# A two-part table of w1's last rows, loaded straight into the matmul operand, in a conv and mixture-of-experts kernel

## The chip, the cores and the metric

The kernel runs on one core of a Trainium2 chip. Its engines work side by side, each on its own row of instructions: PE (TensorE, matmuls), DVE (VectorE), ACT (ScalarE), POOL (GpSimd) and SP (SyncE, which here only issues DMAs). The metric is the device time of one execution in microseconds, as the median of several runs. Beside the runs stands one profiled execution, whose trace gives the rows of this document.

## What is computed

Shapes: x is (8, 2880, 192), so 23040 tokens of 192 values; `w_group` (192, 4), `w_expert` (4, 192, 4), `w1` (4, 4, 192, 1024), `w2` (4, 4, 1024, 192), all float32. Cut to what matters, the reference is:

```python
w = softmax(weight_gen)                        # 8 heads, 7 taps per token
x = einsum('bshk,bskhg->bshg', w, windows(x))  # causal convolution, then (23040, 192)
g = argmax(x @ w_group)                        # one of 4 groups per token
e = argmax(x @ w_expert[g])                    # one of 4 experts in it
h = maximum(x @ w1[g, e], 0)
out = p_group * p_expert * (h @ w2[g, e])      # the two softmax values of the choice
```

Every token goes to exactly one of 16 experts.

## The kernel before

**The front.** The tokens lie in 180 columns of 128, in 15 groups of 12. For each chunk of 6 columns DVE computes the softmax of the taps (L265 `m`, L267 and L268 for the exponential, L273 to L279) and the products of the convolution (L294 `pr`), and sums them (L312, L330); in the first six chunks PE sums part of them by matmuls with the identity (L335), which ACT takes out of PSUM (L338 `xrow`). Then come the router's logits (PE L392, L393, L375, L419; ACT L385 `rem`, L399 `xT`, L411, L422 `ls`), the choice of group and expert on DVE (from L346 `mxg` to L449 `oh`; ACT L352 for the exponentials), the ranks of tokens within an expert (PE L459, L460), and the scatter of each token's row into the DRAM table `rows` by POOL (L503, a DMA per column).

**The blocks.** After certain groups (14 rounds) DVE builds a table that names for each block the rows and the expert. A block takes tokens of one expert. The first ten are plain (128 tokens, float32 matmuls); then come two-unit blocks of 256 tokens; after the last group ten wide blocks of 384, six of 256 and two plain ones. For each block SP loads the rows (`xb`, L779), w1 (L790 for plain blocks: two DMAs straight into the operand `wa`; L792 and L799 for the others) and w2 (`wc`, L803). PE transposes `xb` (L872, L881, L882), multiplies with w1 (L907, the first gemm) and w2 (L945 and L947, L948, the second); ACT takes relu (`hh`, L913; L918 for the split form) and the output (`y`, L954); POOL scatters `y` to the output (L962).

**Split operands.** In blocks that are not plain a float32 operand is written as a rounded high half and a low half in the type float32r, and the gemm is a sum of products of halves. w1 has 192 rows per expert. Its first 128 are loaded as `raw0` (512 KB); ACT casts them into part 0 of `wa` (L816) and DVE writes the difference into part 1 (L840). Part 2 of `wa` holds the last 64 rows twice: 64 partitions with the high half, 64 with the low half. Before the change it is made from `raw1`, to which SP loads 64 rows of w1 and 64 rows of the DRAM table `w1lo` (two DMAs of 256 KB, L799), by one ACT cast (L825, function `split`, part 2).

**The table.** `w1lo` is built in the opening, while the front runs, by the generator `halves` (L595 to L620), pair by pair of experts, k = 0 to 7. For each pair SP fetches the 2 x 64 rows (two DMAs of 256 KB, L610) into a tile that is not yet needed otherwise (parts of `wa`, `wc` and raw tiles); ACT writes minus the high half into another such tile (L602); SP writes the raw tile to `w1lo` (512 KB, L604); POOL adds the negative high half to it with an accumulating DMA (L605). The steps are placed in the program at the planned times `HALVES`, 36 to 78 us; the fetch of pair k stands ahead of the write of pair k-1.

**What sets the order.** Within PE, ACT, DVE and SP the order is that in which the program is written: a planner with a cost for each step steps through blocks (`blocks`) and, where its clock says there is room, through the front and `halves`. An engine takes its row in order, so an instruction that waits holds up all behind it. SP's DMAs also share eight completion counters in turn, so that each waits for the one eight places ahead of it on SP to land. Rings of tiles (three of `wa`, four of `wc`, two each of `raw0` and `raw1`, one `raw2` for w2 of the split blocks) make a load wait until the last reader of that tile is done. `ask(n, part)` puts a load on the list of wanted ones (part 0 `xb`, 1 and 2 w1, 3 w2), `pump` issues them, `pieces(n)` lists a block's ACT casts. The low halves of relu (`hl`, written behind L918 in the split blocks) lie in six pieces of the front's `pr` tiles, taken in turn, so the front has to be complete before the first such block.

## Time and profile before

| | |
|---|---|
| runs | 1208.67, 1213.08, 1214.5 us |
| median | 1213.08 us |
| profiled execution | 1211.98 us |
| its span on the core | 1210.3 us |
| mean granted clock of PE | 0.983 of full speed |
| PE busy | 1135.7 us, 94% of the span |
| DVE busy | 961.3 us, 79% |
| ACT busy | 651.7 us, 54% |
| POOL busy | 571.1 us, 47% |
| DMA | 275.08 MB, mean 227 GB/s |

The profile's page gives busy times of each engine, the span in 40 slices, the chain of work that ended last, and groups of instructions by line; the trace behind it answers narrower questions (what an engine waited for, a timeline of one engine, busy times in given windows). The span is the time from the first to the last instruction on the core; the execution's own time is 1.7 us longer. A name like L825 is a line of the kernel before.

### The profile page before, as it was taken

How to read it: one execution, taken by the hardware profiler on the slowest of the kernel's cores; microseconds unless marked ns; L12 is line 12 of the kernel's file. 1: busy time of each engine (PE TensorE's matmuls, PEld its weight loads, DVE VectorE, ACT ScalarE, POOL GpSimd, SP SyncE). 2: the span in 40 equal slices, each digit the busy share in tenths (PEclk: the TensorE clock that was granted, in tenths of full speed). 3: DMA queues.
4: the chain of work that ended last, by engine and by line, in shares of the span. 5: the costliest groups of instructions: out<-in, count | busy, mean ns of one | idle time of the engine just before them, and what ended most of it. 6: DMA issues, size and time to landing. Idle time of an engine off the chain costs nothing.

```text
span 1210.3 us, 24473 instructions
## 1 busy us (share of the span) xinstructions
PE 1135.7 (94%) x8357; PEld 1078.7 (89%) x8357; DVE 961.3 (79%) x1646; ACT 651.7 (54%) x1235; POOL 571.1 (47%) x608
## 2 busy tenths in 40 slices
PE   5787798999999999999999999999999899999995
PEld 2444788999999999999999999999999899999995
DVE  8899887999998999899999899897625656665560
ACT  1332344655655655655665655555556666666651
POOL 6154182846174747675647664475654112222221
PEclk9998898999999999999999999999999999999998
DMA  5797699787878877888787878649687755555660
GB/s 170 223 303 224 226 298 311 221 296 230 255 252 263 275 238 226 278 261 258 215 283 249 265 223 292 198 129 296 199 275 229 218 155 157 159 163 161 196 204 17
DMA packets 82758, 275.08 MB, mean 227 GB/s; under 512 B 15063, under 2 KB 31734, under 8 KB 80832
## 3 DMA queue, kind: packets, MB, share of 16 engines
q1 hardware_dynamic: 62296, 229.76, 60.9%
q0 software_dynamic: 20208, 43.39, 11.4%
q8 instruction: 67, 1.10, 0.4%
q14 instruction: 67, 0.55, 0.2%
q10 hardware_dynamic: 120, 0.28, 0.1%
HBM read 225.83 MB, written 48.42 MB: 227 GB/s over the span
## 4 chain that ended last, share of the span: by engine, by line
PE 59%; issue 20%; DVE 7%; DMA 6%; POOL 4%; ACT 1%; SPq 1%; POOLq 1%; DVEq 0%; ACTq 0%
PE py L945 26%; PE ph L907 25%; POOL out L962 4%; DVE pr L294 3%; PE pl L375 2%; DMA wt<-in_weight_gen 1%; DMA out<-y,xb 1%; PE tpx L882 1%; PE tpx L881 1%; DMA w1lo<-raw 1%; PE ph L335 1%; DMA raw<-w1lo 1%; PE tp L392 1%; DMA xin<-in_x 1%; DMA raw<-in_moe_w 1%
## 5 line engine op out<-in xcount | busy, mean ns | idle before, releaser
L907 PE MATMUL ph<-xh,wa 128*128 128x256 f32 (+1 forms) x1992 | 466.2, 307 | 0.0
L962 POOL DMA_INDIRECT out<-y,xb x189 | 208.1, 1101 | 445.6 <-DVE y L960 202.5
L945 PE MATMUL py<-wc,hh 128*128 128x192 f32 x2160 | 402.1, 327 | 3.2 <-ACT y L954 3.2
L907 PE MATMUL ph<-xl,wa 128*128 128x256 f32 (+1 forms) x1328 | 360.6, 290 | 0.0
L945 PEld LDWEIGHTS py<-wc,hh 128*128 128x128 f32 x2160 | 348.4, 191 | 3.4 <-ACT y L954 3.4
L907 PEld LDWEIGHTS ph<-xh,wa 128*128 128x128 f32 x1992 | 338.1, 190 | 3.3 <-issue 1.8
L913 ACT ACTIVATE hh<-ph 128x512 f32<-128x512 f32 (+2 forms) x296 | 165.4, 560 | 265.9 <-PE ph L907 265.8
L294 DVE TENSOR_TENSOR pr<-xin,wt 128x1152 f32<-128x1152 f32 x186 | 249.2, 1352 | 5.5 <-PE py L335 3.5
L907 PEld LDWEIGHTS ph<-xl,wa 128*128 128x128 f32 x1328 | 252.3, 190 | 0.4 <-DVE xl L840 0.3
L503 POOL DMA_INDIRECT rows<-xrow,ix x156 | 224.7, 1441 | 47.3 <-POOL ix L502 34.5
L312 DVE TENSOR_TENSOR xrow<-xrow,pr 128x1152 f32<-128x1152 f32 x144 | 194.9, 1353 | 0.7
L840 DVE SCALAR_TENSOR_TENSOR pr<-ph,hh 128x384 fp32r<-128x384 f32 (+1 forms) x128 | 77.6, 607 | 101.7 <-ACT hh L918 100.6
L840 DVE TENSOR_TENSOR wa<-raw,wa 128x1024 fp32r<-128x1024 f32 x83 | 101.5, 1223 | 33.1 <-ACT wa L816 31.4
L947 PE MATMUL py<-wc,hh 128*128 128x384 f32 x352 | 111.9, 365 | 0.0
L918 ACT ACTIVATE hh<-ph 128x384 fp32r<-128x384 f32 (+1 forms) x128 | 68.5, 535 | 73.9 <-PE ph L907 73.9
L502 POOL COPY ix<-posi 128x1 int32<-128x1 int32 x156 | 71.8, 472 | 66.6 <-DMA rows<-xrow,ix 39.3
L816 ACT CAST wa<-raw 128x1024 fp32r<-128x1024 f32 x83 | 87.2, 1050 | 4.2 <-DMA raw<-in_moe_w 4.2
L948 PE MATMUL py<-wc,pr 128*128 128x192 f32 x352 | 88.5, 251 | 0.0
L825 ACT CAST wa<-raw 128x1024 fp32r<-128x1024 f32 x83 | 86.7, 1044 | 0.4 <-DMA raw<-w1lo 0.4
L954 ACT ACTIVATE y<-py,xb 128x192 f32<-128x192 f32 x179 | 67.3, 423 | 22.1 <-PE py L945 20.4
L840 DVE TENSOR_TENSOR xl<-tpx,xh 128x512 fp32r<-128x512 f32 (+1 forms) x94 | 61.7, 656 | 17.2 <-ACT xh L887 16.1
L948 PEld LDWEIGHTS py<-wc,pr 128*128 128x128 f32 x352 | 67.8, 193 | 0.0
(178 smaller groups left out, 1343.5 us busy)
## 6 DMA issues: line engine op xcount, KB each, us to landing
wc<-in_moe_w SPq DMA_DIRECT2D x73, 768.0 KB
raw<-in_moe_w SPq DMA_DIRECT2D x83, 512.0 KB
xin<-in_x SPq DMA_DIRECT2D x14, 1728.0 KB
raw<-in_moe_w SPq DMA_DIRECT2D x91, 256.0 KB
raw<-w1lo SPq DMA_DIRECT2D x83, 256.0 KB
raw<-in_moe_w SPq DMA_DIRECT2D x22, 768.0 KB
xb<-rows SPq DMA_DIRECT2D x72, 194.0 KB
wa<-in_moe_w SPq DMA_DIRECT2D x24, 384.0 KB
```

The source lines that it names most:

```text
L294: nc.vector.tensor_tensor(out=dst, in0=o.xin[:, c0 + k:c0 + k + SC, :].rearrange("p s (h g) -> p s h g", g=HG), in1=w4[:, c0:c0 + SC, :, k ...
L312: nc.vector.tensor_tensor(out=acc, in0=acc, in1=prs[k - 2], op=ALU.add)
L503: written_once(nc.gpsimd.indirect_dma_start(out=rows[:, :], out_offset=bass.IndirectOffsetOnAxis(ap=ix, axis=0), in_=src, in_offset=None, ...
L816: nc.scalar.copy(out=o.wa[:, 0, :], in_=o.raw[0])
L825: nc.scalar.copy(out=o.wa[:, 2, :], in_=o.raw[1])
L840: f(*a, **k)
L907: nc.tensor.matmul(ph[:, v, :], lhsT=w[:, f0:f0 + P], rhs=rhs, start=i == 0, stop=i == len(terms) - 1)
L913: nc.scalar.activation(out=hh, in_=ph, func=AF.Relu)
L945: nc.tensor.matmul(b.acc[t], lhsT=hh[:, v, c], rhs=wc[0][:, f, :], start=f == 0 and not (b.wide and t == 1), stop=f == NFT - 1 and not (b. ...
L947: nc.tensor.matmul(b.py[t], lhsT=hh[:, v, c], rhs=wc[f // 4][:, f % 4].rearrange("p l d -> p (l d)"), start=f == 0, stop=False)
L948: nc.tensor.matmul(b.acc[t], lhsT=hl[:, v, c], rhs=wc[f // 4][:, f % 4, 0, :], start=False, stop=f == NFT - 1)
L962: ins = nc.gpsimd.indirect_dma_start(out=out[:, :], out_offset=bass.IndirectOffsetOnAxis(ap=b.x.bitcast(I32)[:, t, D + 1:D + 2], axis=0), ...
```

## The change

The DRAM table becomes `w1s`, with two parts of 64 rows for each expert: part 0 the rounded high half, part 1 the low half. For each pair `halves` now makes two casts on ACT (minus the high half, then the high half, L592 of the changed kernel), writes each in two DMAs of 256 KB, one for each expert (L595), and adds the raw rows to the low part by two accumulating DMAs on POOL (L597), whose target is of type float32r. More tiles serve as places meanwhile: all three `wa`, the four `wc`, both `raw0` and one of the former raw2. A non-plain block loads the 128 x 1024 of both parts with one DMA of 512 KB straight into part 2 of `wa` (L789); L825 and the ring `raw1` go. That load is asked for at the end of block n for block n+3 (for the third block of all in the lead) and not behind the casts of the block two ahead, and its tile is free when PE has done the first gemm of block n. `hl` gets a ring of four tiles of its own, and the front is forced to completion only ahead of wide split blocks.

```diff
-    w1lo = dram.tile([NE, HP, F], F32, name="w1lo")
+    w1s = dram.tile([NE, 2, HP, F], F32, name="w1s")
...
-    hls = []
-
-    def new_hl():
-        if not hls:
-            for _ in range(3):
-                t = cv.tile([P, 2, 2, BK], F32R, name="pr", bufs=3)
-                hls.extend(t[:, k] for k in range(2))
-        hls.append(hls.pop(0))
-        return hls[-1]
-
-    new_raw = [ring(f"raw{i}", m, [P, n]) for i, (n, m) in enumerate(((F, 2), (F, 2), (NFT * D, 1)))]
+    new_raw = [ring(f"raw{i}", m, [P, n]) for i, (n, m) in enumerate(((F, 2), (NFT * D, 1)))]
+    new_hl = ring("hl", 4, [P, 2, BK], F32R)
...
-        def lower_half(k):
-            e, hi, raw = 2 * k, his[k % len(his)], raws[k]
-            nc.scalar.activation(out=hi, in_=raw, func=AF.Copy, scale=-1.0)
-            low = w1lo[e:e + 2].rearrange("e p f -> (e p) f")
-            nc.sync.dma_start(out=low, in_=raw)
-            nc.gpsimd.dma_start(out=low, in_=hi.bitcast(F32), accum_op=ALU.add)
-            run("pool", 1.1, run("act", 1.0))
+        spare, third, other = [wp.tile([P, 3, F], F32, name="wa", bufs=3) for _ in range(3)]
+        raws = [t[:, k, :] for t in (spare, third) for k in range(3)] + [new_raw[0]() for _ in range(2)]
+        first3 = [other[:, k, :] for k in range(3)]
+        rest5 = [wp.tile([P, NFT, D], F32, name="wc", bufs=4).rearrange("p f d -> p (f d)")[:, 0:F] for _ in range(4)]
+        rest5.append(new_raw[1]()[:, 0:F])
+        parts = [t.bitcast(F32R) for t in 2 * first3 + 2 * rest5]
+
+        def divide(k):
+            for q, scale in enumerate((-1.0, 1.0)):
+                part = parts[2 * k + q]
+                nc.scalar.activation(out=part, in_=raws[k], func=AF.Copy, scale=scale)
+                run("act", 1.0)
+                for h in range(2):
+                    nc.sync.dma_start(out=w1s[2 * k + h, 1 - q], in_=part.bitcast(F32)[h * HP:(h + 1) * HP, :])
+            for h in range(2):
+                nc.gpsimd.dma_start(out=w1s.bitcast(F32R)[2 * k + h, 1], in_=raws[k][h * HP:(h + 1) * HP, :], accum_op=ALU.add)
+            run("pool", 2.2, clk["act"])
...
-            for h, src in enumerate((w1v[bass.ds(o.ev, 1), P:D, :], w1lo[bass.ds(o.ev, 1), :, :])):
-                nc.sync.dma_start(out=o.raw[1][h * HP:(h + 1) * HP, :], in_=src.rearrange("o p f -> p (o f)"))
+            nc.sync.dma_start(out=new_wa(o, F32R).bitcast(F32)[:, 2, :], in_=w1s[bass.ds(o.ev, 1)].rearrange("o l p f -> (o l p) f"))
...
-        elif part == 2:
-            nc.scalar.copy(out=o.wa[:, 2, :], in_=o.raw[1])
-            o.tw = max(o.tw, run("act", 0.95))
...
-        return [(1, 1), (2, 1)] + ([] if whole(n) else [(3, 0), (3, 1)])
+        return [(1, 1)] + ([] if whole(n) else [(3, 0), (3, 1)])
...
-            if not o.whole:
+            if b.wide and not o.whole:
                 while step() is not False:
                     pass
...
             if plain(n):
                 ask_w(n)
+            else:
+                ask(n, 2)
             ask_x(n)
...
-                if end and n + 3 < n1 and (plain(n + 3) or plain(n + 2)):
-                    ask_w(n + 3)
-                    if not plain(n + 3):
-                        ask_w(n + 4)
+                if end and n + 3 < n1:
+                    if plain(n + 3):
+                        ask_w(n + 3)
+                    else:
+                        ask(n + 3, 2)
+                        if plain(n + 2):
+                            ask(n + 3, 1)
+                            ask(n + 4, 1)
```

On SP, the building of the table in the opening (targets of L610 are places for fetched rows; here the fetches of pairs 4, 5 and 6 and the writes of pairs 3, 4 and 5) stood thus in the kernel before:

```order
L610 DMA raw_190<-in_moe_w 64x1024 x2
L604 DMA w1lo<-wc 128x1024
L610 DMA raw_189<-in_moe_w 64x1024 x2
L604 DMA w1lo<-raw_190 128x1024
L610 DMA raw_192<-in_moe_w 64x1024 x2
L604 DMA w1lo<-raw_189 128x1024
```

and stands thus in the changed one, where L602 is the fetch (pairs 5, 6 and 7) and L595 the write (pairs 4 and 5):

```order
L602 DMA wa<-in_moe_w 64x1024 x2
L595 DMA w1s<-wc 64x1024 x4
L602 DMA raw_190<-in_moe_w 64x1024 x2
L595 DMA w1s<-raw_191 64x1024 x2
L595 DMA w1s<-wc 64x1024 x2
L602 DMA raw_189<-in_moe_w 64x1024 x2
```

One write per pair, from the fetched tile, has become four from the tiles that ACT writes, and each fetch stands behind them.

On ACT, between the logits' copies of the second chunk (L399) and the evacuation of the third chunk's sums (L338), before:

```order
L399 COPY xT<-tp 128x384
L602 ACTIVATE wc<-raw_190 128x1024
L602 ACTIVATE wc<-raw_189 128x1024
L602 ACTIVATE wc<-raw_192 128x1024
L338 COPY xrow<-py_584 128x2x192
L338 COPY xrow<-tpx 128x2x192
L338 COPY xrow<-ph_586 128x2x192
```

and after, where the lines are L390, L592 and L329:

```order
L390 COPY xT<-tp 128x384
L592 ACTIVATE wc<-wa 128x1024 x2
L592 ACTIVATE raw_191<-wa 128x1024
L592 ACTIVATE wc<-wa 128x1024
L592 ACTIVATE wc<-raw_190 128x1024 x2
L329 COPY xrow<-py_607 128x2x192
L329 COPY xrow<-tpx 128x2x192
L329 COPY xrow<-ph_609 128x2x192
```

Ahead of the third chunk's evacuation there are six casts, of pairs 4, 5 and 6, where there were three.

On SP, at the first two-unit block (block 10: `raw_189`; block 11: `raw_190`), before:

```order
L792 DMA raw_189<-in_moe_w 128x1024
L799 ISA
L799 DMA raw_191<-in_moe_w 64x1024
L799 ISA
L799 DMA raw_191<-w1lo 64x1024
L787 TENSOR_LOAD tab_1368
L787 ISA x2
L792 ISA
L792 DMA raw_190<-in_moe_w 128x1024
```

and after, where L783 loads the first 128 rows and L789 the table:

```order
L789 ISA
L789 DMA wa<-w1s 128x1024
L783 ISA
L783 DMA raw_189<-in_moe_w 128x1024
L778 TENSOR_LOAD tab_1411
L778 ISA x2
L783 ISA
L783 DMA raw_190<-in_moe_w 128x1024
```

The table's load for block 10, with `wa` as its target, has come ahead of `raw_189`, and the two loads to `raw_191` and `raw_192` are gone. At the end of the table's building, pair 7's write (behind the second plain block's loads) has become four writes; its tiles are no longer parts of the `wa` that the third plain block's load takes.

## Rows read from the trace of the kernel before

**Rows 1.** The page: busy time of each engine over the span

```profile
PE 1135.7 (94%) x8357; PEld 1078.7 (89%) x8357; DVE 961.3 (79%) x1646; ACT 651.7 (54%) x1235; POOL 571.1 (47%) x608
```

**Rows 2.** Windows: busy us of each engine (instructions), granted clock, DMA share, GB/s

```profile
60.00:90.00 30.00, 25.04 (x123) 13.90 (x122) 27.34 (x41) 11.82 (x22) 16.80 (x16) 0.94 1.04 305
...
300.00:840.00 540.00, 539.89 (x4271) 532.69 (x4271) 496.87 (x840) 318.05 (x594) 308.24 (x295) 1.00 0.78 248
840.00:1140.00 300.00, 291.85 (x2028) 285.28 (x2027) 171.28 (x334) 183.97 (x342) 98.35 (x117) 0.99 0.64 192
```

**Rows 3.** What PE waits for, 125 to 215 us: total, times, longest

```profile
PE py L945 <- ACT y L954: 3.2, 1, 3.2
PE pl L459 <- DVE oh L449: 3.0, 1, 3.0
```

**Rows 4.** The page's groups: busy, mean ns of one, idle before, releaser

```profile
L825 ACT CAST wa<-raw 128x1024 fp32r<-128x1024 f32 x83 | 86.7, 1044 | 0.4 <-DMA raw<-w1lo 0.4
```

**Rows 5.** Timeline of PE, 960 to 968 us: start, duration, what [idle before]

```profile
966.54 0.45 PE L881 MATMUL tpx<-ident,xb 128*128 128x128 f32 x1 [3.47 <-DVE xl L840]
```

**Rows 6.** Timeline of ACT in the opening

```profile
47.99 1.06 ACT L602 ACTIVATE wa<-wa 128x1024 fp32r<-128x1024 f32 x1
...
67.88 2.01 ACT L602 ACTIVATE wc<-raw 128x1024 fp32r<-128x1024 f32 x2
...
76.67 0.48 ACT L338 COPY xrow<-py 128x384 f32<-128x384 f32 x1 [5.54 <-PE py L335]
...
83.40 0.36 ACT L422 COPY ls<-pl 128x240 f32<-128x240 f32 x1 [0.64 <-PE pl L419]
```

**Rows 7.** The chain of work that ended last: start, duration, what

```profile
83.67 1.36 DVE pr L330
...
100.07 11.14 DMA w1lo<-raw
...
111.77 5.96 DMA w1lo<-wa
...
120.66 6.72 DMA wt<-in_weight_gen
```

**Rows 8.** Timeline of SP (its DMA issues), pairs 3 to 6 of the table

```profile
49.73 1.29 SPq L610 DMA_DIRECT2D wc<-in_moe_w  x2
...
55.05 0.34 SPq L604 DMA_DIRECT2D w1lo<-wc  x1
55.43 1.39 SPq L610 DMA_DIRECT2D raw<-in_moe_w  x2
...
60.65 1.66 SPq L610 DMA_DIRECT2D raw<-in_moe_w  x2
65.97 0.34 SPq L604 DMA_DIRECT2D w1lo<-raw  x1
...
70.05 0.34 SPq L604 DMA_DIRECT2D w1lo<-raw  x1
```

**Rows 9.** Timeline of SP around the third plain block's load

```profile
111.90 1.51 SPq L779 DMA_DIRECT2D xb<-rows  x2
117.93 0.90 SPq L790 DMA_DIRECT2D wa<-in_moe_w  x2
```

**Rows 10.** Timeline of DVE, 121 to 129 us

```profile
127.41 0.85 DVE L265 TENSOR_REDUCE m<-wt 128x96 f32<-128x672 f32 x1 [4.92 <-DMA wt<-in_weight_gen]
```

**Rows 11.** Windows at the two places where PE has stood

```profile
143.00:149.00 6.00, 5.97 (x26) 5.93 (x26) 5.62 (x25) 1.26 (x4) 1.18 (x3) 0.50 0.00 1
198.00:200.00 2.00, 1.60 (x5) 1.60 (x6) 1.97 (x7) 1.64 (x4) 0.97 (x1) 0.50 1.05 284
```

**Rows 12.** Timeline of SP at the first two-unit block

```profile
186.97 0.33 SPq L792 DMA_DIRECT2D raw<-in_moe_w  x1
```

**Rows 13.** Timeline of ACT at the first two-unit block

```profile
196.45 1.04 ACT L816 CAST wa<-raw 128x1024 fp32r<-128x1024 f32 x1 [4.20 <-DMA raw<-in_moe_w]
```

**Rows 14.** Timeline of PE: block 7's last first-gemm group

```profile
188.88 1.06 PE L907 MATMUL ph<-xd,wa 96*128 96x128 f32 x8
```

21 lines of the change are left out of this document (6 added, 15 removed).

## The prediction

> **What bounds the kernel now.** I read the busy times of the engines first, then a table of windows, then who waits for whom where TensorE (PE) stands, then the queues around those places. ScalarE (ACT), which the change relieves most, is busy 54% of the span, PE 94% [rows 1]. From 300 to 840 us PE is busy 539.89 of 540 us, and from 840 to 1140 us 291.85 of 300 [rows 2]: in these 840 us all of PE's gaps together are 8.3 us, and work taken from ACT or from the queues can win no more than that there. The gaps lie before 300 us. From 60 to 90 us PE is busy 25 of 30 us, VectorE (DVE) 27.34, and the DMA engines are full at 305 GB/s [rows 2]: this opening is a chain on DVE with the DMA rings full beside it. What the change can do to the time is decided by the opening, and by two places where PE stands about 3 us each: at 143.03 us for DVE's `oh`, and at 198.40 us for ACT's `y` [rows 3].
>
> A warning on this reading. The Trainium skill's page "Perfetto Trace Analysis" (section "Identifying the Most-Contended Engine") says that busy matmuls are no good measure of the headroom of TensorE, and that one should look at the busy share of its weight loads. By that column PE is loading 532.69 of 540 us here, so that up to 7 us would be open, and 6.6 us more from 840 to 1140. By my reading the term for these stretches is nothing; by the page's it is bounded by -14 us, all of it won. I stay with the row of PE, since the list of its waits names almost nobody there; the page's case is among the rivals.
>
> **What goes: 83 casts and 83 loads.** Each non-plain block loses L825, 1044 ns on ACT, 86.7 us in all [rows 4]. ACT has the room, and PE doesn't wait for it from 300 us on, so this counts nothing where PE is full; the cover is PE's own work. It counts where a block stands just behind such a cast: at 966.54 us, the one large stop late in the kernel, PE waits 3.47 us for `xl` behind DVE [rows 5]; L825 goes shortly ahead of the ACT steps that DVE waits for there, but most of the 3.5 us is L816, the subtraction and the wide block's first preparation. I take -0.2, with 0 and -1.0 as ends (the whole cast). The two 256 KB loads of a block become one of 512 KB: the bytes are the same, the issues on SP fewer.
>
> **What the opening pays.** Per pair k of experts the table now costs two ACT casts (before one), four writes of 256 KB on SP (before one of 512 KB) and two accumulating DMAs on POOL (before one): 8 casts, 24 SP DMAs, 8 POOL DMAs and 4 MB of writes more. The casts lie on ACT, 1.06 us each [rows 6], which is nowhere full; the POOL DMAs stand between scatters that keep pace with the rows, and I put them at nothing, with 2 us as the other end if the last scatter of the first table slips. What matters is order. Before, SP wrote a raw tile as soon as it was fetched; now a write waits for the cast on ACT, and SP asks for the fetch of pair k+2 behind the writes of pair k. So the even pairs form a chain: two casts (2.1 us), four issues (about 1.5 us), a fetch of L us, again. Pair 0's casts can begin where ACT has its first one now, at 47.99 us [rows 6]. Pair 6's then begin at 48.0 + 3 x (3.6 + L) and end 2.1 us later, and behind them in ACT's order stands the evacuation of the third chunk's sums, now at 76.67 us [rows 6]. Behind that are the logits, out at 83.40 + 0.36 = 83.76 us [rows 6], and DVE takes them when its L330 ends at 83.67 + 1.36 = 85.03 us [rows 7]: 1.27 us of slack. The delay of the DVE chain is thus D = 48.0 + 10.8 + 3L + 2.1 - 76.67 - 1.27 = 3L - 17, not less than about 0.7, since pair 4's casts don't begin before 67.88 us [rows 6].
>
> L is read from SP's rows, from the issue of a fetch to the write that waits for its landing: 49.73 to 55.05 (5.3 us), 55.43 to 65.97 (10.5) and 60.65 to 70.05 (9.4) [rows 8]. At L = 5.3 D is 0.7, at 10.5 it would be 14.5. I take L = 7.5, somewhat under the mean of the three (8.4), because SP now stands while ACT casts, and the rings are emptier when the fetch is asked for; against that, 1 MB of writes is queued just ahead of it, which with its own 0.5 MB is 5.2 us at the 305 GB/s of [rows 2]. So D = 5.5, between 0.7 and 10. Everything behind (the first table, the scatters, the first plain loads) shifts by D; there is no idle time of DVE to take it up before 127 us.
>
> **What the stop at 143 us gives back.** Pair 7's write, issued at 100.07, takes 11.14 us to land, its accumulation from 111.77 another 5.96 [rows 7]. The third plain block's load goes to the tile that this accumulation reads, so SP, which has issued `xb` at 111.90, stands until 117.93 [rows 9]; behind it is the load of `wt` at 120.66, 6.72 us to land [rows 7], for which DVE stands 4.92 us until 127.41 [rows 10]. That ends in the 3.0 us for which PE stands before 143.03 [rows 3], and PE then runs from 143 to 149 at a granted clock of 0.50, 1.2 of its 2.4 GHz [rows 11]: it does in 6 us what takes half of that at full clock. After the change pair 7's parts lie in other tiles, so the load may go right behind `xb`, at about 113.5: 4.4 us earlier, and `oh` with it (DVE is free 4.9 us before it starts). PE itself is ready for `oh` 3.0 us earlier. So the stop of 3.0 us goes, and with it about 3.3 us of half clock: -6.3. If only half of that is won (PE late itself, clock low for another reason) it is -3.
>
> **What the first two-unit block pays.** `raw0` of block 10 is issued at 186.97 [rows 12] and ACT's cast of it starts at 196.45, after 4.20 us of waiting for it [rows 13]; `hh`, `xd` and `y` stand behind the cast and PE behind `y` (3.19 us, [rows 3]). In the new order `w1s` of block 10 comes ahead of `raw0`, and it waits on SP for PE's last first-gemm group of block 7, at 188.88 to 189.9 [rows 14]. The rings are full there (1.05, 284 GB/s from 198 to 200, [rows 11]), so the later issue itself costs little, but 512 KB stand ahead that did not: 0.52 / 284 = 1.8 us. I take +1.8; 0 if the backlog drains earlier, +3 if the issue (2.9 us later) counts in full. The Trainium skill's "DMA: Bandwidth & Descriptors" (section "Bandwidth") measured 341 GB/s for a transfer of 1 MB: by that the same 512 KB are 1.5 us and the sum 0.3 less; the row is slower, and I keep it.
>
> **Later blocks.** `w1s` of block n+3 is asked for when block n ends and waits for the tile that block n's first gemm gives up. The slowest landing read above took 11.14 us [rows 7], and two blocks lie between the request and the need (83 non-plain blocks in the thousand us behind 200 are some twelve us each): nothing. If the cover were gone, each of 83 blocks would pay. The four tiles of `hl` cost nothing: the front's steps stand in the same order until the first group's last blocks.
>
> **Sum** against the profiled execution, 1211.98 us (span 1210.3): +5.5 - 6.3 + 1.8 - 0.2 = +0.8. The median of the three runs is 1.1 us above the profiled one, so 1213.08 + 0.8 = 1213.9, rounded to 1214.
>
> **Rivals.** (1) Slower: the opening. SP, ACT and the fetches go round in a circle, and ACT stands on pair 6's fetch in front of the evacuation. The place is the third chunk, the price D - 4.7 in all (the other terms as above), and it is slower by more than 6 us from D = 10.8, or L = 9.3. For it: two of the three fetches read took longer than that, and 4 MB are added to full rings (13 us at 305 GB/s). Against: fewer bytes are in flight, since no more than a pair's writes stand ahead. L = 9.3 to 10.5 gives +6.2 to +9.8, say 1221. (2) Faster: the opening costs 1 us, since the fetches are short, and the stop at 198 us goes too, because SP is no longer 4.4 us late and has one request less in the way: +1 - 6.3 - 3.2 and half of another 3.3 us of half clock (the window from 198 to 200 is at 0.50), so -10, to about 1204. For it: both stops hang on late loads; against: `raw0` stands behind a wait for PE that it did not have. (3) The page's case: PE's weight loads gain from a freer ACT over 840 us. All of it would be -14, to about 1200; against it, PE waits for no ACT step there. (4) The change doesn't bite late: a `w1s` load lands after its block starts. 0.5 us in each of 83 blocks is +41, about 1255; against it stand two blocks of lead. (5) Nothing moves, because D eats just what the stop gives: that is inside the forecast.
>
> **How the numbers follow.** Forecast, with D between 0.7 and 10 and its neighbours at their ends: 1207 to 1219, chance 0.58. Rival 1: 0.23. Rival 2: 0.14. Rival 3: 0.02. Rival 4: 0.03. 0.5%, about what a measurement of this kernel can tell from no change, is 6 us, so faster means under 1207 and slower over 1219. Faster: rivals 2 and 3 and the low end of the forecast, 0.18. Slower: rivals 1 and 4, 0.26. The range reaches from the low end of the forecast to rival 1's end: 1206 to 1222.
>
> **What would show it.** In the profile after: pair 6's two casts on ACT shortly ahead of the third chunk's evacuation, at 81 to 84 us instead of 70; `mxg` of that chunk about 5 us late; SP not standing between `xb` and the third plain load; no wait of PE for `oh` behind it and no 0.50 there; at the first two-unit block a wait of PE for `y` of about 5 us; PE full from 300 to 840 us as before; no L825. It would be wrong if the third chunk's evacuation hardly moves (then faster), if DVE waits for `xin` or scatters in the opening, if the stop at 143 us merely changes its cause, or if PE waits for `w1s` in block after block.

## The result and the profile after

The changed kernel takes 1221.65 us (median of 4 runs, 1221.13 to 1225.47) against 1210.88 us for the kernel before (4 runs, 1206.98 to 1214.50): a ratio of 1.0103 with a 95% interval of 1.0063 to 1.0142. It is slower by about 1%, some 11 us. Its profiled execution took 1222.01 us, with a span of 1220.3 us and a mean granted clock of 0.975. One kept profile, that of c_before among the experiments, is of an execution slower than the others of its kernel (1257.85 us); only its opening is used below.

Both traces hold the same number of matmuls in the same order. The start of a matmul after minus its start before says how late the changed kernel runs at that point (median of 15 neighbours; times are those of the kernel before, all in us):

| at | 70 | 95 | 113 | 130 | 158 | 220 | 320 | 880 | 935 | 1173 |
|---|---|---|---|---|---|---|---|---|---|---|
| delay | +2.7 | +14.0 | +13.6 | +20.8 | +13.4 | +13.7 | +12.5 | +12.2 | +13.0 | +9.8 |

So some 14 us are lost before 100 us, 7 more between 113 and 130 that are given back by 158, next to nothing changes up to 935, and 3 come back near the end. The page and the table of windows of the changed kernel say the same. First the page's line of busy times (busy us, share of the span, instructions), then the windows, with the columns of [rows 2].

```profile
PE 1137.0 (93%) x8357; PEld 1079.9 (88%) x8357; DVE 959.0 (79%) x1646; ACT 589.4 (48%) x1160; POOL 599.2 (49%) x616
```

```profile
60.00:90.00 30.00, 17.51 (x70) 9.46 (x68) 25.47 (x24) 12.47 (x17) 24.24 (x21) 0.90 0.98 286
...
155.00:161.00 6.00, 6.00 (x47) 5.65 (x46) 5.76 (x18) 1.75 (x7) 1.07 (x1) 1.00 0.84 285
212.00:217.00 5.00, 5.00 (x21) 5.00 (x21) 4.66 (x26) 0.39 (x1) 2.71 (x6) 0.50 0.71 184
300.00:840.00 540.00, 540.00 (x4273) 533.05 (x4273) 495.76 (x824) 277.79 (x546) 314.21 (x296) 1.00 0.73 248
840.00:1140.00 300.00, 291.91 (x2048) 288.00 (x2047) 177.88 (x353) 164.67 (x320) 118.70 (x124) 0.99 0.60 195
```

ACT has lost 62 us of work in all [rows 1] and PE is exactly as full from 300 to 840 us as before [rows 2]. From 60 to 90 us, where PE was busy 25 of 30 us, it is now busy 17.5; and although the change adds 4 MB to the opening, the DMA engines move less than before, 286 GB/s where it was 305, at a busy share of 0.98 where it was 1.04 [rows 2].

**The opening.** The next two fences are ACT and SP of the changed kernel (start, length, engine, line, operation, how many in a row, and in brackets the idle time before and what ended it). L592 are the casts, L602 the fetches, L595 the writes of the table.

```profile
48.03 2.95 ACT L592 ACTIVATE wa<-wa 128x1024 fp32r<-128x1024 f32 x3
...
58.50 1.06 ACT L592 ACTIVATE wa<-wa 128x1024 fp32r<-128x1024 f32 x1 [4.04 <-DMA wa<-in_moe_w]
...
71.17 2.00 ACT L592 ACTIVATE wc<-wa 128x1024 fp32r<-128x1024 f32 x2 [0.51 <-DMA wa<-in_moe_w]
80.36 1.06 ACT L592 ACTIVATE raw<-wa 128x1024 fp32r<-128x1024 f32 x1 [7.19 <-DMA wa<-in_moe_w]
...
88.23 2.00 ACT L592 ACTIVATE wc<-raw 128x1024 fp32r<-128x1024 f32 x2 [5.86 <-DMA raw<-in_moe_w]
90.14 0.46 ACT L329 COPY xrow<-py 128x384 f32<-128x384 f32 x1
```

```profile
59.05 2.14 SPq L602 DMA_DIRECT2D wa<-in_moe_w  x2
61.29 3.66 SPq L595 DMA_DIRECT2D w1s<-wa  x4
65.00 1.96 SPq L602 DMA_DIRECT2D wa<-in_moe_w  x2
67.06 4.26 SPq L595 DMA_DIRECT2D w1s<-wc  x4
71.36 4.38 SPq L602 DMA_DIRECT2D wa<-in_moe_w  x2
75.83 4.38 SPq L595 DMA_DIRECT2D w1s<-wc  x4
80.26 2.50 SPq L602 DMA_DIRECT2D raw<-in_moe_w  x2
...
110.11 0.87 SPq L781 DMA_DIRECT2D wa<-in_moe_w  x2
...
130.03 1.49 SPq L770 DMA_DIRECT2D xb<-rows  x2
132.50 0.89 SPq L781 DMA_DIRECT2D wa<-in_moe_w  x2
```

Pairs 0, 2, 4 and 6 have their casts at 48.03, 58.50, 71.17 and 88.23: cycles of 10.5, 12.7 and 17.1 us. ACT stands 7.19 us for pair 5 and 5.86 for pair 6, together 13.05, and behind both stands the evacuation of the third chunk, at 90.14 instead of 76.67 [rows 6], 13.5 us late. SP's row has no gap of more than 0.25 us from 59 to 82 us: a DMA of 256 KB takes it 0.9 to 2.2 us there, as the mean of a row (4.38 us for four), against 0.4 for each of the two of the load at 110. The first plain load goes out at 110.11 instead of 95.92, 14.2 us late.

**The waits behind it.** These are rows of the lists of who waited for whom (total us, times, longest), PE from 95 to 215 us and DVE from 60 to 180.

```profile
PE tp L859 <- DMA xb<-rows: 3.9, 1, 3.9
PE py L932 <- ACT y L941: 3.1, 1, 3.1
```

```profile
DVE mxg L337 <- ACT ls L413: 11.4, 1, 11.4
...
DVE m L256 <- DMA wt<-in_weight_gen: 0.5, 1, 0.5
```

DVE stands 11.4 us for the logits of the delayed chunk. `xb` comes 18.1 us late (130.03 against 111.90, [rows 9]), so PE waits 3.9 us for it: with the late scatters ahead of `xb` this is where the extra microseconds between 113 and 130 arise. DVE's wait for `wt` is 0.5 us where it was 4.92 [rows 10], and the third plain load follows `xb` at once.

**Late in the kernel.** Waits of PE's weight loads from 1000 to 1160 us, first of the kernel before, then of the changed one:

```profile
PEld tpx L881 <- DVE xl L840: 2.2, 7, 0.3
```

```profile
PEld tpx L868 <- DMA xb<-rows: 0.4, 1, 0.4
PEld tpx L869 <- ACT xd L852: 0.3, 1, 0.3
```

Seven waits of 0.3 us for `xl` are gone. The delay falls by 3.2 us from 935 to 1173, 0.9 of them at the stop of [rows 5] and 2.3 in the wide blocks behind it, where these waits were. PE's own row doesn't show them: from 840 to 1140 us it is busy 291.85 us before and 291.91 after, while the weight loads go from 285.28 to 288.00 [rows 2].

### The profile page after: what moved, and what is told of

It is laid out like the page before. It is cut to its first block, busy times and chain, and to the rows that moved or that the text cites. A ratio compares the mean times of both kernels' runs of the same rounds, so it can differ in the third digit from the quotient of the medians.

```text
span 1220.3 us, 24204 instructions
## 1 busy us (share of the span) xinstructions
PE 1137.0 (93%) x8357; PEld 1079.9 (88%) x8357; DVE 959.0 (79%) x1646; ACT 589.4 (48%) x1160; POOL 599.2 (49%) x616
## 3 DMA queue, kind: packets, MB, share of 16 engines
q0 software_dynamic: 20336, 43.40, 10.8%
## 4 chain that ended last, share of the span: by engine, by line
PE 78%; DMA 7%; issue 6%; DVE 2%; ACT 2%; SPq 2%; POOL 1%; POOLq 0%; ACTq 0%; DVEq 0%
PE ph L894 34%; PE py L932 28%; PE py L934 3%; PE pl L366 2%; DMA w1s<-wc 2%; PE py L935 2%; PE tpx L869 1%; PE tpx L868 1%; DMA xb<-rows 1%; POOL out L949 1%; PE pl L934 1%; DVE pr L285 1%; DMA raw<-in_moe_w 1%; SPq L595 1%; PE tp L383 1%
## 5 line engine op out<-in xcount | busy, mean ns | idle before, releaser
L949 POOL DMA_INDIRECT out<-y,xb x189 | 226.1, 1196 | 410.8 <-DVE y L947 181.0
L932 PEld LDWEIGHTS py<-wc,hh 128*128 128x128 f32 x2160 | 347.6, 191 | 3.3 <-ACT y L941 3.3
L285 DVE TENSOR_TENSOR pr<-xin,wt 128x1152 f32<-128x1152 f32 x186 | 249.2, 1350 | 11.8 <-PE py L326 10.4
L827 DVE SCALAR_TENSOR_TENSOR hl<-ph,hh 128x384 fp32r<-128x384 f32 (+1 forms) x128 | 77.6, 606 | 99.2 <-ACT hh L905 99.2
L806 ACT CAST wa<-raw 128x1024 fp32r<-128x1024 f32 x83 | 87.2, 1050 | 4.4 <-DMA raw<-in_moe_w 4.4
L935 PE MATMUL py<-wc,hl 128*128 128x192 f32 x352 | 88.6, 252 | 0.0
L935 PEld LDWEIGHTS py<-wc,hl 128*128 128x128 f32 x352 | 67.7, 192 | 0.0
L934 PEld LDWEIGHTS py<-wc,hh 128*128 128x128 f32 x352 | 66.8, 190 | 0.5
```

The costliest lines, as they stand in the source:

```text
L285: nc.vector.tensor_tensor(out=dst, in0=o.xin[:, c0 + k:c0 + k + SC, :].rearrange("p s (h g) -> p s h g", g=HG), in1=w4[:, c0:c0 + SC, :, k ...
L806: nc.scalar.copy(out=o.wa[:, 0, :], in_=o.raw[0])
L827: f(*a, **k)
L932: nc.tensor.matmul(b.acc[t], lhsT=hh[:, v, c], rhs=wc[0][:, f, :], start=f == 0 and not (b.wide and t == 1), stop=f == NFT - 1 and not (b. ...
L934: nc.tensor.matmul(b.py[t], lhsT=hh[:, v, c], rhs=wc[f // 4][:, f % 4].rearrange("p l d -> p (l d)"), start=f == 0, stop=False)
L935: nc.tensor.matmul(b.acc[t], lhsT=hl[:, v, c], rhs=wc[f // 4][:, f % 4, 0, :], start=False, stop=f == NFT - 1)
```

## The experiments

The kernels ran on several chips, and these differ: on three of the chips the kernel before takes 1237 to 1242 us, on the others 1208 to 1211. Each ratio is against the kernel before on the same chip, so ratios count only among kernels of one chip. What can be compared across all of them is the opening, which the control shows: the kernel before itself, run among the experiments on one of the slower chips (c_before), has the third chunk's evacuation at 76.08 us and its matmuls within 2.3 us of the first trace from 113 to 158 us. The table gives the time of that evacuation (76.67 in the rows of before) and the delay of PE at four points as above, always against the profiled execution of before.

| kernel | evacuation | at 113 | at 130 | at 158 | at 220 | before on that chip | ratio, 95% interval |
|---|---|---|---|---|---|---|---|
| c_before | 76.08 | -0.3 | 0.0 | -2.3 | – | 1236.97 | |
| e_swap | 75.61 | -1.8 | +1.7 | -4.1 | -2.6 | 1241.83 | 0.9993 (0.9959 to 1.0028) |
| e_bytes | 77.02 | -1.3 | +4.6 | +1.2 | -0.8 | 1241.83 | 0.9998 (0.9960 to 1.0036) |
| e_lead | 83.29 | +7.7 | +15.3 | +9.4 | +10.8 | 1241.83 | 0.9998 (0.9969 to 1.0027) |
| e_whole | 84.80 | +7.3 | +16.5 | +9.1 | +10.4 | 1241.83 | 1.0090 (1.0057 to 1.0123) |
| c_after | 88.45 | +12.0 | +24.6 | +17.2 | +19.6 | 1236.97 | 1.0023 (0.9985 to 1.0061) |
| e_sign1 | 81.23 | +5.1 | +12.8 | +5.4 | +11.8 | 1236.97 | 0.9951 (0.9917 to 0.9985) |
| e_sign2 | 76.78 | +0.1 | +6.1 | -1.0 | +1.6 | 1236.97 | 0.9889 (0.9831 to 0.9946) |
| e_sign2b | 76.16 | -0.6 | +5.5 | +1.5 | +4.4 | 1208.40 | 0.9978 (0.9953 to 1.0003) |
| e_sign3 | 80.99 | +3.8 | +15.6 | +8.1 | +9.2 | 1208.40 | 1.0009 (0.9988 to 1.0030) |
| e_sign4 | 76.95 | +0.3 | +1.1 | -4.9 | -1.4 | 1208.40 | 0.9993 (0.9959 to 1.0027) |
| e_hl | 89.23 | +12.1 | +21.4 | +13.9 | +12.1 | 1208.40 | 1.0105 (1.0069 to 1.0141) |
| e_cast | 101.26 | +24.7 | +24.7 | +21.5 | +26.8 | 1236.67 | 1.0126 (1.0060 to 1.0192) |
| e_raw0 | 74.58 | -2.0 | -2.0 | -2.7 | -0.3 | 1236.67 | 0.9976 (0.9940 to 1.0012) |
| e_sign5 | 77.62 | +1.1 | +4.7 | -1.5 | -4.6 | 1236.67 | 0.9950 (0.9909 to 0.9992) |
| e_sign6 | 77.42 | -1.0 | +6.8 | -0.2 | +1.2 | 1236.67 | 0.9975 (0.9938 to 1.0011) |
| e_sign5b | 76.90 | -0.3 | +5.0 | -1.4 | -2.0 | 1209.65 | 0.9920 (0.9896 to 0.9945) |
| c_after2 | 89.20 | +12.3 | +20.2 | +13.6 | +13.3 | 1209.65 | 1.0115 (1.0081 to 1.0149) |

The theory to test: the table's second half, with the pieces that it is written in, makes a circle of ACT, SP and the fetches in front of the third chunk. Its rivals: the added 4 MB in full rings; SP's wait for ACT by itself; and a loss elsewhere (the direct load, `hl`).

### The wait, the bytes and the lead

e_lead is the changed kernel with each fetch asked for up to two pairs further ahead:

```diff
-            fetch(k)
+            for m in range(3) if k == 0 else range(k + 2, min(k + 3, len(raws))):
+                fetch(m)
```

> The changed kernel with one thing moved: the fetches of the raw rows run two pairs further ahead (fetch of pair k+2 instead of pair k ahead of the writes of pair k-1). Same bytes, same casts, same writes. If the loss is the circle fetch - casts on ACT - writes on SP - next fetch, the casts of pairs 4 to 6 find their rows there, the third chunk's evacuation starts at 78 to 83 us (76.67 before the change, 90.14 after), the first plain load at 97 to 102 us (95.92; 110.11), and the time is 1210 to 1215 us. If the loss is the 4 MB of extra writes in full DMA rings, the evacuation still starts at 86 us or later and the time is 1218 to 1223 us.

e_bytes and e_swap are the kernel before, with one trait of the changed one each: 4 MB more written (a second copy of the raw rows to a table that nobody reads), and SP's write waiting for ACT's cast.

```diff
...
             nc.sync.dma_start(out=low, in_=raw)
+            nc.sync.dma_start(out=extra[e:e + 2].rearrange("e p f -> (e p) f"), in_=raw)
```

> The kernel before with the bytes alone: each pair's raw rows are written a second time, to another DRAM table that nobody reads (512 KB per pair, 4 MB in all, 8 SP DMAs more, no new wait for ACT). If the loss is the order, the third chunk's evacuation starts at 76 to 80 us and the time is 1210 to 1214 us. If it is the bytes, the first plain load moves from 95.9 to 105 us or later and the time is 1218 to 1223 us.

```diff
-            nc.sync.dma_start(out=low, in_=raw)
-            nc.gpsimd.dma_start(out=low, in_=hi.bitcast(F32), accum_op=ALU.add)
+            nc.sync.dma_start(out=low, in_=hi.bitcast(F32))
+            nc.gpsimd.dma_start(out=low, in_=raw, accum_op=ALU.add)
```

> The kernel before with the wait alone: SP writes ACT's cast (minus the high half) instead of the raw rows, and POOL adds the raw rows to it; the sum in the table is the same, so are bytes and counts, but each write, and every fetch behind it, now waits for ACT. If the order is the loss, the third chunk's evacuation starts at 78 to 86 us and the time is 1212 to 1218 us; a single cast and one write per pair make it shorter than in the changed kernel. If the bytes are it, nothing moves: 76 to 78 us and 1208 to 1213 us.

The evacuation of the third chunk in the three kernels (ACT's timeline; of e_lead with the last cast ahead of it):

```profile
82.33 1.06 ACT L592 ACTIVATE wc<-raw 128x1024 fp32r<-128x1024 f32 x1 [3.58 <-DMA w1s<-wc]
83.29 0.46 ACT L329 COPY xrow<-py 128x384 f32<-128x384 f32 x1
```

```profile
77.02 0.46 ACT L339 COPY xrow<-py 128x384 f32<-128x384 f32 x1
```

```profile
75.61 0.46 ACT L338 COPY xrow<-py 128x384 f32<-128x384 f32 x1
```

Neither the bytes alone nor the wait alone delays the opening: 77.02 and 75.61 us, where it was 76.67. The bytes come through only later, as 4.6 us at 130, of which 1.2 are left at 158. So a rival falls that the prediction itself had used as an argument, 4 MB in full rings. (Each of the two came out in the branch that its expectation had kept for the other cause. Both together with a single cast were not tried.) The lead brings 5 to 7 of 13 us back and no more, because the casts now wait for something else: pair 6's second cast stands 3.58 us until the write that reads its tile has landed. The fetch was one side of the circle, the places are the next.

### Pieces, and the second cast

e_whole is the changed kernel with two tables, one for the high and one for the low halves, so that a pair's part is written by one DMA of 512 KB over 128 partitions. A block then loads its part 2 by two DMAs.

```diff
...
-                for h in range(2):
-                    nc.sync.dma_start(out=w1s[2 * k + h, 1 - q], in_=part.bitcast(F32)[h * HP:(h + 1) * HP, :])
-            for h in range(2):
-                nc.gpsimd.dma_start(out=w1s.bitcast(F32R)[2 * k + h, 1], in_=raws[k][h * HP:(h + 1) * HP, :], accum_op=ALU.add)
+                nc.sync.dma_start(out=w1s[1 - q, 2 * k:2 * k + 2].rearrange("e p f -> (e p) f"), in_=part.bitcast(F32))
+            nc.gpsimd.dma_start(out=w1s.bitcast(F32R)[1, 2 * k:2 * k + 2].rearrange("e p f -> (e p) f"), in_=raws[k], accum_op=ALU.add)
...
```

> The changed kernel with the table laid out as two tables of 16 x 64 rows, so that a pair's part is written by one DMA of 512 KB instead of two of 256 KB (and added to by one on POOL); a block's load becomes two DMAs of 256 KB, still straight into the operand. Same bytes, same order, 16 SP DMAs fewer in the opening. If SP's issues are what makes the circle long (an issue waits for the DMA eight places ahead of it), the third chunk's evacuation starts at 80 to 86 us and the time is 1213 to 1219 us. If the bytes or the landing time of a fetch are it, the evacuation stays at 88 to 91 us and the time at 1220 to 1223 us.

SP's writes of the table from the `wc` tiles, in the changed kernel and in e_whole (how many; shortest, median and longest in ns; first and last start in us):

```profile
L595 SPq DMA_DIRECT2D w1s<-wc x16: 499/882/3442, 67.1 to 114.8; - x16
```

```profile
L594 SPq DMA_DIRECT2D w1s<-wc x8: 337/338/397, 64.0 to 107.9; - x8
```

ACT of e_whole:

```profile
77.05 1.06 ACT L592 ACTIVATE raw<-wa 128x1024 fp32r<-128x1024 f32 x1 [6.57 <-DMA wa<-in_moe_w]
...
82.89 2.00 ACT L592 ACTIVATE wc<-raw 128x1024 fp32r<-128x1024 f32 x2 [3.83 <-DMA raw<-in_moe_w]
84.80 0.46 ACT L329 COPY xrow<-py 128x384 f32<-128x384 f32 x1
```

A pair's writes, the same 1 MB, take SP two issues of 0.34 us instead of the 4.38 us of the four at 75.83, SP's row is no longer solid, and the evacuation comes about 5 us earlier. The Trainium skill's "DMA: Bandwidth & Descriptors" (section "Rules for kernel authors") says that two transfers to the two halves of the partitions don't run side by side and one over 128 partitions should be used; no row here shows whether the halves run side by side, but one DMA over 128 partitions is the better choice here too, and the rows show its price on the issuing side. The other 8 us of delay are still there.

What these two kernels gain in time can't be read off: on one chip, and with nearly the same delay from 158 to 320 us, e_lead has a ratio of 0.9998 and e_whole one of 1.0090. What tells them apart lies behind 320 us and isn't explained.

e_sign1, e_sign2 and e_sign3 take the second cast away as well. One cast makes minus the high half; the raw rows are written first and it is added to them, which leaves the low half as before the change; and the table's high part holds minus the high half, made good by a negated copy of x's last 64 values in `xd`. In e_sign2 SP writes the raw rows whole and POOL the rest, with two tables as in e_whole; e_sign1 keeps one table in pieces with SP writing the high half a pair later; e_sign3 is in pieces too, with POOL writing the high half. Of e_sign2:

```diff
...
+            nc.scalar.activation(out=his[k], in_=raws[k], func=AF.Copy, scale=-1.0)
...
+            nc.sync.dma_start(out=low, in_=raws[k])
+            nc.gpsimd.dma_start(out=low, in_=his[k].bitcast(F32), accum_op=ALU.add)
+            nc.gpsimd.dma_start(out=high, in_=his[k].bitcast(F32))
...
-        nc.scalar.copy(out=b.xd, in_=b.x[:, :, P:D].unsqueeze(2).broadcast_to([P, b.nt, 2, HP]))
+        for h, sign in enumerate((-1.0, 1.0)):
+            nc.scalar.activation(out=b.xd[:, :, h, :], in_=b.x[:, :, P:D], func=AF.Copy, scale=sign)
```

> The changed kernel with a table that needs one cast per pair: part 0 holds minus the high half, part 1 the low half, and the blocks negate the first of the two copies of x's last 64 columns (one more short ACT copy per block). SP writes the raw rows first, as before the change, without a wait for ACT; ACT's cast is written by SP one pair later; POOL adds it to the raw rows. Same 4 MB more of writes and the same direct load as in the changed kernel. If the loss is that SP stands behind ACT in the opening, the third chunk's evacuation is back at 76 to 79 us, the third plain load is free of pair 7, and the time is 3 to 10 us under the kernel before (ratio 0.992 to 0.998). If the direct load in the blocks costs something itself, it is at or over the kernel before (1.000 to 1.006).

> The same table content, laid out as two tables, with whole writes: SP writes the raw rows of a pair in one DMA of 512 KB, POOL adds minus the high half to them and also writes it to the other table; a block's load is two DMAs of 256 KB. SP's row in the opening is that of the kernel before. If SP behind ACT is the loss, the opening is as before the change and the ratio 0.992 to 0.999. If the two loads of a block instead of one matter (the run with whole writes was no faster than the changed kernel), this run is slower than the one with a single load by 5 us or more.

> The same kernel as the run with one cast, two tables and whole writes, beside its variants and the kernel before on one chip: ratio 0.985 to 0.997; chunk 3's evacuation at 76 to 78 us. If its 0.9889 was a chance of few runs, 0.997 to 1.003.

> One cast per pair and POOL writing the upper part, as in the run with two tables, but in the changed kernel's single table, so that a block loads it with one DMA of 512 KB and the table costs 256 KB pieces again (8 SP DMAs and 24 POOL DMAs more than with two tables). If the pieces in the opening decide, the third chunk's evacuation or the first scatters come 3 to 8 us later than with two tables and the time is 3 to 8 us over it. If the single load of a block decides, the late blocks and the middle win 5 to 10 us and it is that much under it.

e_cast goes the other way: e_sign2 with the second cast put back (16 parts in 8 places), and both parts sent by POOL, so that SP waits for no cast.

> Two tables and whole writes, SP writing the raw rows without a wait for ACT, as in the run with one cast per pair, but again two casts per pair (minus the high half and the high half, both written by POOL; x's copies not negated). If the second cast alone delays the opening (it stands on ACT ahead of the third chunk's evacuation and waits for the places of earlier parts), the evacuation starts at 79 to 85 us and the time is 3 to 9 us over that run (ratio to before 1.001 to 1.006). If it takes the cast together with SP's wait for it, the evacuation is at 76 to 79 us and the ratio 0.995 to 1.000.

The evacuation in e_sign2b (the run of e_sign2 on the faster kind of chip), and the last casts and the evacuation in e_cast:

```profile
76.16 0.48 ACT L329 COPY xrow<-py 128x384 f32<-128x384 f32 x1 [2.11 <-PE py L326]
```

```profile
60.06 1.06 ACT L594 ACTIVATE wa<-wa 128x1024 fp32r<-128x1024 f32 x1 [9.45 <-DMA w1s<-wa]
...
96.52 1.06 ACT L594 ACTIVATE wc<-wa 128x1024 fp32r<-128x1024 f32 x1 [17.77 <-DMA w1s<-wc]
...
101.26 0.46 ACT L329 COPY xrow<-py 128x384 f32<-128x384 f32 x1
```

With one cast and whole writes the opening is that of the kernel before, although the 4 MB and the direct load are there: ACT even waits 2.11 us for PE ahead of the evacuation. One cast in pieces costs 4 to 5 us (80.99 and 81.23; e_sign1 had been expected at 76 to 79), two casts in whole writes 8, two casts in pieces 12 to 13.5. The two costs add up. (In e_sign2 SP also no longer waits for ACT. That wait by itself costs nothing, as e_swap showed; whether it adds to the 8 us beside a second cast isn't separated.) e_cast, which was expected at 79 to 85 us and came at 101, shows that the second cast can cost much more than its 1.06 us, and without a wait of SP for it: it is worse there, because each place is used twice, and the cast that uses it again stands until POOL's DMA of the first use has landed, 9.45 and 17.77 us. e_cast changes where the parts are sent from as well, so its 25 us are no measure of the second cast in the changed kernel; that the second use of a place waits is common to it and to e_lead.

That the late opening is also the lost time is seen best on the chip where e_hl (the changed kernel but for `hl`, see below), e_sign3 (one cast, pieces) and e_sign2b (one cast, whole writes) ran side by side: they are 12.1, 3.8 and -0.6 us late at 113, and their medians are 1222.42, 1210.11 and 1207.60 us, where the kernel before takes 1208.40. The last two end some 4 us sooner for a reason of their own (the end of POOL's row, further down); without it the first step is about 8 us, like that of the opening, and the second is 2.5 us as it stands. e_sign2's 0.9889, from four runs on a slower chip, did not come again: 0.9978, inside what the second expectation called a chance of few runs.

### `hl`, and what was left behind the opening

e_hl is the changed kernel with `hl` in the front's tiles again, as in the kernel before.

```diff
-    new_hl = ring("hl", 4, [P, 2, BK], F32R)
...
+                t = cv.tile([P, 2, 2, BK], F32R, name="pr", bufs=3)
+                hls.extend(t[:, k] for k in range(2))
...
-            if b.wide and not o.whole:
+            if not o.whole:
```

> The changed kernel with one part undone: the low halves of relu again in pieces of the front's tiles. If L825's loss is what frees the late blocks, nothing moves: no wait of PE's weight loads for xl from 1000 to 1160 us (2.2 us before the change, none after), and the time is that of the changed kernel, ratio 1.000 to 1.012. If the own tiles are what frees them, the 2.2 us are back and the time is 2 to 4 us more.

Its ratio is 1.0105, the changed kernel's own. Its waits for `xl` late in the kernel are gone too, so neither the loss nor the late gain hangs on `hl`.

Four kernels take e_sign2 further. e_sign4 puts the last pair 46 us later in the plan (`Until(HALVES[-1] + 52.0)` for `+ 6.0`), since pair 7's megabyte goes out next to the second chain of scatters; e_sign5 also asks for `raw0` of the first two-unit block a block earlier; e_sign6 is e_sign5 with the last pair in its old place; and e_raw0 is the kernel before with that early `raw0` alone.

```diff
+                    if n + 4 < n1 and plain(n + 3) and not plain(n + 4):
+                        ask(n + 4, 1)
```

> The run with two tables with one thing moved: pair 7's cast, writes and addition come about 46 us later in the plan (behind the third plain block's and the next front chunk's loads). If 1.5 MB for pair 7 in full rings is what makes the first rows (xb) of the plain blocks land late (PE 6 us late there with two tables, made good at the stop that follows), the first block starts 2 to 6 us earlier and the time is 1 to 5 us under it; if those us are made good anyway, the same within 1 us.

> One cast per pair, two tables, pair 7 late, and the first 128 rows of block 10's w1 asked for one block earlier (ahead of block 9's xb and wc on SP). If the stop of 6.3 us at the first two-unit block is that request's place, PE waits there for y 0 to 3 us, the half clock behind it goes, and the ratio is 0.988 to 0.995. If the rings' fill decides, 5 us or more remain and the ratio is 0.996 to 1.001.

> As the run before it, with pair 7 in its old place: if pair 7's place doesn't count in the end, the same ratio as that run within 0.2%; if it does, 2 to 5 us more.

> The kernel before with only the load of block 10's first 128 rows asked for one block earlier. If the place of the request makes the stop of 3.2 us at 198 us and the half clock behind it, both go: 3 to 6 us less, ratio 0.995 to 0.998. If not, 1.000.

> The version with one cast per pair, two tables, pair 7 late and block 10's rows asked for earlier, once more with more rounds: ratio to before 0.990 to 0.997 as on the first chip; if that was the chip's middle stretch, 0.997 to 1.002.

What PE waits for near the first two-unit block in e_sign2b, then e_sign4, then e_sign5b (the run of e_sign5 with more rounds, on the faster kind of chip):

```profile
PE py L931 <- ACT y L940: 5.7, 1, 5.7
```

```profile
PE py L931 <- ACT y L940: 6.3, 1, 6.3
```

```profile
PE tpx L867 <- DMA xb<-rows: 2.0, 1, 2.0
```

Where the opening isn't late, the wait for `y` is 5.7 and 6.3 us instead of 3.19 [rows 3]; this fits the direct load's place ahead of `raw0`. With `raw0` asked for earlier it is gone (as it is in e_raw0, without a direct load). The last pair's place matters less than was hoped: e_sign4 is 4 to 6 us ahead of e_sign2b from 130 us on, but its ratio, 0.9993 with runs from 1199.90 to 1217.05, shows no gain, and e_sign5 and e_sign6, with it and without it, can't be told apart (0.9950 and 0.9975, intervals that overlap). Nor can e_raw0 be told from the kernel before.

e_sign5b takes 1201.31 us against 1209.65: 0.9920 (0.9896 to 0.9945), faster than both kernels. Its PE from 300 to 840 us is as full as the others':

```profile
300.00:840.00 540.00, 540.00 (x4274) 533.06 (x4273) 495.24 (x840) 283.21 (x597) 309.95 (x297) 1.00 0.77 249
```

But about half of its gain has nothing to do with how blocks load the table. In its profile it is 3.6 us early at the last matmul and 7.6 us early at the end of the span. What differs behind the last matmul is the end of POOL's row, first in the kernel before, then in e_sign5b (how many; shortest, median and longest in ns; first and last start in us):

```profile
L1172 POOLq DRAIN  x3: 46/109/7710, 1201.8 to 1210.0; - x3
```

```profile
L1165 POOLq DRAIN  x3: 46/109/4443, 1197.5 to 1202.5; - x3
```

The longest of these, the instruction named DRAIN behind the last scatter, takes 7.7 us in every kernel here in which all of POOL's DMAs to the table add (the kernel before, the changed one, e_whole, e_sign1 and the others), and 4.4 to 4.6 us in every one in which POOL also writes the high half with plain DMAs (e_sign2 to e_sign6, e_cast). With the instruction ahead of it, these kernels end 3.6 to 4.1 us sooner behind their last matmul than the others. Why is not shown. e_sign2b, 0.7 us late at its last matmul, owes its 0.9978 to this too.

So loading the table straight into the operand can win, but of the 8.3 us here only some 4 are left for it (0.4%, with 3 us to either side by the interval), if the table is made with one cast and whole writes and the first two-unit block gets its `raw0` in time. How much each of these brings isn't resolved by the intervals.

### The changed kernel again, on two chips

> The kernel before, for its trace on the chip of these runs: ratio 1.000, third chunk's evacuation at 76 to 77 us, first plain load at 95 to 96 us, PE's two stops at 143 and 198 us. On another chip than that of the first trace the stretch from 300 to 840 us may not be full of PE.

> The changed kernel itself on the chip of these runs, so that the experiments are compared with it and not over chips: ratio 1.006 to 1.014 as first measured, the third chunk's evacuation near 90 us and the first plain load near 110 us. If a chip's own delays in the middle of the kernel differ between the two kernels, the ratio differs while the opening does not.

> The changed kernel beside it: ratio 1.002 to 1.012, the third chunk's evacuation at 87 to 92 us on any chip.

c_after2 repeats the result (1.0115). On the slower kind of chip the loss shrinks to 1.0023 (c_after, expected at 1.006 to 1.014), with an opening just as late (88.45). There PE is not full in the middle: from 300 to 840 us it is busy 529.34 us in e_swap, and its largest wait has no releaser (windows, then PE's waits in that stretch):

```profile
300.00:840.00 540.00, 529.34 (x4091) 516.21 (x4090) 475.07 (x790) 304.22 (x570) 297.20 (x285) 0.99 0.74 236
```

```profile
PE pl L375 <- issue: 6.5, 14, 1.1
```

The matmuls themselves are longer as well: 4091 in 529.34 us are 129 ns each, the changed kernel's 4273 in 540.00 us 126. Between 320 and 880 us the profiled executions on the slower chips lose 13 us (c_after) to 29 us (e_swap) to the first trace, one execution of each, and kernels with the table of before (e_raw0 18, e_bytes 20) don't stand apart from the others (e_lead 19, e_whole 25). What makes the smaller ratios is therefore open, and the ratios of the slower chips are not set against those of the others.

## Why the prediction came out as it did

The forecast was 1214 us, about no change; it became 1221.65, which is the number of the first rival (1221) by that rival's mechanism: SP, ACT and the fetches in a circle, ACT standing on pair 6's fetch in front of the evacuation, no pair or place beside those that it named. That the number agrees so closely is partly luck: the rival priced everything but the opening at -4.7 us, and it came to -4.4, but out of other parts (see the end of this section). The likeliest case was mis-sized at one step of the opening, and the gain that it set against the opening was used up elsewhere.

**The opening: wrong in size, +5.5 foreseen, +13.5 measured.** Its formula was two casts, four issues and a fetch, three times round. The first round held (58.50 against 59.1), the second was a little long (71.17 against 70.2), the third took 17.1 us instead of 11.1. Its parts by SP's and ACT's rows: casts 2.0 (as foreseen); then SP is still in the fetch of pair 5 until 75.74, 2.6 us after the casts' end at 73.17; the four issues take 4.4; the fetch, from 80.26 to 88.21, takes 8.0 (7.5 foreseen). So the step that failed is "four issues (about 1.5 us)": they and the two of the other pair ahead of them took 7.0. The formula let the even pairs turn in a circle of their own, but SP serves the odd ones in between, and in this stretch each of its issues took about three times what was assumed. L, on which the text spent its bounds, was off by only 0.5 us. The rounds before gave 1 us more, and the 1.3 us of slack that were subtracted weren't there: the first plain load is 14.2 us late, the evacuation 13.5.

The rows of before held a warning. In them SP's fetch and write rows [rows 8] were read for their landings alone. Two issues of 256 KB in a row take 1.29 to 1.66 us there, which is 2.6 to 3.3 for four; 1.5 is about what four of the whole writes take (0.34 each). With 3.0 instead of 1.5 the formula gives a delay of 10.0 us instead of 5.5; what is missing from there is SP's work for the other pair. The issues went into the sum at one value, with no second end. The Trainium skill's page "Perfetto Trace Analysis" (section "What "DMA-bound" means") counts a solid row of DMA slices on the issuing engine as a bound of its own beside the DMA engines. SP's row from 59 to 82 us is such a row, and the 286 GB/s are less than the 305 of before; but the DMA engines are busy for 0.98 of that stretch too, so the trace alone doesn't say which of the two holds the other up.

The first rival had the mechanism but reached its price through L of 9.3 to 10.5, which isn't what happened, and its argument of 4 MB in full rings fell with e_bytes.

**Scatters and POOL's DMAs: 0, with 2 as the other end; wrong for a while.** The second chain of scatters is late by 14.9 us (last one at 124.00 against 109.08) and `xb` behind it by 18.1. Last scatter to `xb` is 6.0 us instead of 2.8. From 113 to 130 the delay grows by 7.2 us; it grows by 5.9 in e_bytes too, which is on time up to 113, so the added bytes alone bring most of it. In e_sign4, where pair 7 goes out later, it grows by 0.8.

**The stop at 143 us: right in itself, but its gain was spent.** From 130 to 158 us the delay falls by 7.4 us (6.3 foreseen): the third plain load stands right behind `xb`, DVE waits 0.5 us for `wt`, and the window 155 to 161 that now answers to [rows 11] has a granted clock of 1.00 instead of 0.50. But it only makes good the passing delay of `xb`: the delay at 158 is that at 113. In e_sign4, where `xb` is hardly late, the delay goes from +0.3 at 113 to -4.9 at 158, so some 5 us are really to be had.

**The first two-unit block: +1.8 foreseen, +0.3 measured; the mechanism shows only elsewhere.** The wait for `y` is 3.1 us as before; the clock falls to 0.50 in 212 to 217 as it did before. That the rings have had time to drain, with everything 13 us late there, is a guess. Where the opening is on time, the wait grows by 2.5 to 3.1 us (e_sign2b, e_sign4), near the upper end given.

**Wide blocks: -0.2 foreseen, end -1.0, about -3.2 measured.** It was looked for at the one stop at 966 us, where 0.9 us go; the rest is seven small waits of the weight loads behind `xl`, which PE's row and the rows chosen didn't show. This is the third rival in small: where the weight loads had gaps, 2.3 us were won although PE's row was full. From 300 to 840 us the weight loads go from 532.69 to 533.05 us only, and next to nothing is won. The later blocks cost nothing, as foreseen: 540.00 us of 540.

In all, by the delays of the trace: 14.2 at the first plain load, -0.8 for scatters and stop together (13.4 at 158 us), +0.3 at the first two-unit block, -1.2 up to 320, +0.5 up to 935 and -3.2 behind it, which is +9.8; the medians give +10.8. Against the forecast's +5.5 - 6.3 + 1.8 - 0.2, the opening was 8.7 us worse, and the stop's gain was 5.5 us smaller for the scatters and `xb` put at nothing. What brings the -1.2 is open.

## What to carry to other kernels

When work that is done in passing (a table, a conversion) gets more and smaller DMAs, count every issue on the queue's engine, those of the neighbouring items too, and bound what one of them takes from a stretch in which many follow each other. An instruction in an in-order engine row that uses a buffer again waits for the DMA that read it; two casts for one, with the same number of places, can cost not 1 us but a landing. A direct load can be worth having even where the version that introduces it loses: find which part loses, here the making of the table, before the idea is dropped. And when a variant wins, see where: half of what the best one won here was in the last microseconds, behind the last matmul.

## What the runs showed of the hardware

- **Issues on SP got longer when DMAs of 64 partitions followed each other:** the table's writes of 256 KB from the `wc` tiles took 0.5 to 3.4 us each in the changed kernel, and SP's issues from 59 to 82 us 1.1 us in the mean (4.38 us for four), where writes of 512 KB over 128 partitions took 0.34 us in e_whole and the two loads of 512 and 256 KB at 110 us 0.87 us together. It is not the bytes: e_whole sends as many. What sets it is open. The guess that an issue waits for the DMA eight places ahead of it isn't borne out: where the trace has its landing, it had landed.
- **More requests, fewer bytes:** from 60 to 90 us the kernels that write the table in 256 KB pieces moved 276 to 297 GB/s (286 in the changed kernel), those that write it in whole pieces 300 to 348 (305 in the kernel before, 312 in e_whole, 341 in e_sign2b). e_cast, whose casts stand for landings, moved 291.
- **POOL's last DRAIN:** 7.7 us where all of POOL's DMAs to the table accumulate, 4.4 to 4.6 us where it also writes plain ones, in every kernel here; the cause is open.
- **Chips of two kinds:** the same kernel before takes 1208 to 1211 us on some and 1237 to 1242 on others. On the first kind PE is full in the middle (539.89 us of 540), in the kernels run on the other it has 6 to 11 us of gaps there, in e_swap most of them with no releaser in the trace, and matmuls of 129 ns where the others have 126. The size of a change of 1% depends on which one it is measured on: 1.0103 and 1.0115 against 1.0023.
